# Block-sparse attention and a routed layer on one core: scores against one buffer of eight key blocks, shared values for 64 queries at once

## The chip, the core and the metric

The kernel runs on one core of a Trainium2 chip. Its engines run their own instruction streams in order: TensorE (PE, with its weight loads shown apart as PEld), VectorE (DVE), ScalarE (ACT), GpSimd (POOL) and SyncE (SP, which issues most of the transfers). The metric is the device time of one execution in microseconds, lower is better; three executions of the kernel before are given, and one of another execution's trace is read.

## The reference, cut to what matters

```python
# q, k, v: (4, 8, 768, 64), blocks of 32: 24 blocks; scale = 1/8
mask = np.abs(blk_i - blk_j) <= 1
mask = mask | (blk_i == 0) | (blk_j == 0) | (blk_i == 23) | (blk_j == 23)
for qb in range(24):
    for kb in sampled_blocks[qb]:                 # three random blocks a query block
        mask[qb * 32:(qb + 1) * 32, kb * 32:(kb + 1) * 32] = True
attn = softmax(np.where(mask, scale * q @ k.T, -1e9))
x = (attn @ v).transpose(0, 2, 1, 3).reshape(4, 768, 512)
# then, for each of the 4 batches: the 128 rows with the highest x @ w_gate
h = np.maximum(x[top] @ w1, 0.0); out[top] = x[top] + sigmoid(score) * (h @ w2)
```

A middle query block sees at most eight key blocks: the two blocks of its own unit, the first and the last block (these four are shared by both query blocks of a unit), and four of its own: three random ones and the outer neighbour. The first and the last query block see all 24.

## The kernel before

Work runs in 28 cycles, 14 for each pair of batches. In a pair, three **group** cycles (u = 0) hold query blocks 0 and 23 against a third of the keys each, and eleven **unit** cycles hold two neighbouring query blocks (e = 0, 1) with all heads of both batches (b = 0, 1). A cycle c on TensorE is, in program order:

- **turn**: 16 products with the identity that turn the probabilities `pr` of cycle c (128 by 128 each) into `ring` banks; ScalarE copies three of the four results to `pt`, VectorE the fourth;
- steps of the routed layer that are due at "m" (`spread`, `columns`, `column_sums`, `choose`, the first product `h`);
- `ahead(c + 1)`: **scores** of the next cycle for b = 0 and 1; VectorE takes their maxima (`m`, then `mx`, or `gx` in a group cycle), ScalarE the exponentials (`pr`);
- **outputs** of cycle c: probabilities (`pt`, the weights of the product) times values (65 columns, the last one is 1 and gives the sum);
- on VectorE `norm` (`z`, `x`, `j`), and the steps due at "e" (`expand` makes `r`, `rank` makes `cmp`, `select`).

Every fp32 product of scores and outputs is two matmuls and two weight loads on TensorE, a product with the identity is one of each. Scores use tiles of 64 by 32 of the array, outputs tiles of 128 by 32 (32 queries). A unit's scores are made of two products: one of 128 shared keys straight from `k` (the array `kb`), one of 128 own keys from `kr`, which GpSimd copies together two cycles ahead (`pool_work`, `keys`: six copies at offsets read from the table `koff`, and one for the neighbours). GpSimd also gathers the rows of own values `vr` by an indirect transfer; shared values `vs` come by SyncE.

The banks of `ring` go round three at a time, two banks each: two for turn, two for scores, one for outputs in each cycle. Small results of the routed layer (`bcast` of `spread`, `turnt`, `sums`, `selp`) share one bank, `tiny`; the order among its writers and readers is kept for the bank as a whole. `table()` and `rows_table()` turn the sampled blocks (`rb_i`) into `koff` and the row indices `vidx` on VectorE. Each engine keeps the order in which the program is written.

Of the kernel before, what the change touches and what calls it, by code (L numbers as in the profile page):

```python
# [7 lines left out]
F32 = mybir.dt.float32  # L8
# [4 lines left out]
ALU = mybir.AluOpType  # L13
# [28 lines left out]
def block_sparse_attention_moe(ctx, tc, qt, kt, vt, blocks, w_gate, w1, w2, outs):  # L42
# [144 lines left out]
    def rows_table():  # L187
# [4 lines left out]
        for pr in range(PAIRS):  # L192
# [14 lines left out]
    lim = const.tile([P, S], F32, name="lim")  # L207
    pool.memset(lim[:, 0:S - P], LIM0)
    limit = const.tile([P, P], F32, name="limit")
    pool.memset(limit, LIM0)  # L210
    pool.affine_select(lim[:, S - P:S], limit, pattern=[[-1, P]], compare_op=ALU.is_gt, fill=LIM,
                       base=0, channel_multiplier=1)
# [15 lines left out]

    krs, vrs, offs = {}, {}, {}

# [15 lines left out]
    def keys(n, e):  # L246
        pr, u = units[n]
        if e == 0:
            krs[n] = inp.tile([P, 2, NP, BP, KW], F32, tag="kr", name=f"kr{pr}_{u}", bufs=2)
        flat = kb[pr].rearrange("p j b c -> p (j b c)")  # L250
        for s in range(3):
            pool.tensor_copy(krs[n][:, e, s].rearrange("p b c -> p (b c)"), flat[:, ds(offs[n][3 * e + s], BP * KW)])
        if e:
            pool.tensor_copy(krs[n][:, :, 3], kb[pr][:, 2 * u - 2:2 * u + 2:3])

    def fetch_keys(n):
        if n < len(units):
            offsets(n)
            for e in range(2):
                keys(n, e)  # L260

# [10 lines left out]

    def grid(k, part, j, step, b, cols):
        a = k[part, j:j + 2, b, cols]
        return bass.AP(a.tensor, a.offset, [a.ap[0], [step * BP * KW, 2], a.ap[1], a.ap[2]])

    def scores(c, b):
        pr, u, t = c
        s = banks().rearrange("p g (h j k) -> p g h j k", h=2, k=BLK)
        q = qs[pr, u]  # L280
        for ph in range(2):
            for part in range(2 if u else 1):
                for e in range(2):
                    for p2 in range(2):
                        p, r0 = 2 * p2 + ph, 64 * p2 + 32 * e
                        cols = slice(p * BLK, (p + 1) * BLK)
                        for g in range(G):
                            half = slice(64 * g, 64 * g + 64)
                            if not u:
                                o, k = slice(0, 8), kb[pr][half, THIRD * t:THIRD * (t + 1), b, cols]  # L290
                            elif part == 0:
                                o, k = slice(0, 4), grid(kb[pr], half, 2 * u - 1, NB - 2 * u, b, cols)
                            else:
                                o, k = slice(4, 8), krs[number[c]][half, e, :, b, cols]
                            pe.matmul(s[r0:r0 + 32, g, ph, o], q[half, b, p, e], k,
                                      start=ph == 0 and part == 0, stop=ph == 1 and (part == 1 or not u),
                                      tile_position=(64 * g, r0), skip_group_check=True)
        return s.rearrange("p g h j k -> p g h (j k)")
# [50 lines left out]

    def outputs(c, b, o):  # L350
        pr, u, t = c
        for n in range(2):
            pt = pts.pop((c, b, n))
            for i in range(NP):
                for e in range(2):
                    for p2 in range(2):
                        h, r0 = p2 * NP + i, 64 * p2 + 32 * e
                        cols = slice(h * VW, (h + 1) * VW)
                        if not u:
                            v = vg[:, 2 * t + n, b, cols]  # L360
                        elif n == 0:
                            v = vss[number[c] % NVS][:, b, cols]
                        else:
                            v = vrs[number[c]][:, e, b, cols]
                        pe.matmul(o[r0:r0 + 32, b, i * VW:(i + 1) * VW], pt[:, i, r0:r0 + 32], v,
                                  start=n == 0 and i == 0, stop=n == 1 and i == NP - 1,
                                  tile_position=(0, r0), skip_group_check=True)

# [100 lines left out]
    def fetch(pr, b):  # L469
        ts = rout.tile([P, 2], F32, tag="ts", name=f"ts{pr}_{b}", bufs=4)  # L470
        vec.tensor_reduce(ts[:, 0:1], selp[:, b, 0:2], AX.X, ALU.add)
        it = R[pr]["it", b] = rout.tile([P, 1], U32, tag="it", name=f"it{pr}_{b}", bufs=4)
        vec.tensor_copy(it, ts[:, 0:1])
        xe = R[pr]["xe", b] = rout.tile([P, DM], F32, tag="xe", name=f"xe{pr}_{b}", bufs=4)
        pool.indirect_dma_start(out=xe[:], out_offset=None, in_=outs[BP * pr + b][:, :],
                                in_offset=bass.IndirectOffsetOnAxis(ap=it[:, 0:1], axis=0))
        vec.tensor_reduce(ts[:, 1:2], selp[:, b, 2:5], AX.X, ALU.add)
        R[pr]["ts", b] = ts
# [46 lines left out]


    n, per = len(cycles), NU + 2
    due = {}
# [17 lines left out]
    for pr in range(PAIRS):  # L546
        for t in range(NT):
            c = pr * per + 2 + 2 * t + 1
            if c == n - 1:
                break  # L550
            at(c, "e", expand, pr, t)
            at(c + 1, "m", spread, pr, t)
            at(c + 2, "m", columns, pr, t)
            at(c + 2, "m", rank, pr, t, 0)
            at(c + 2, "e", rank, pr, t, 1)
            at(c + 3, "m", column_sums, pr, t)
            if t % 2:
                at(c + 3, "p", parts, t - 1, t + 1, pr)
# [17 lines left out]

    done = None
    table()
    rows_table()

    def ahead(c):
# [9 lines left out]
    ahead(cycles[0])  # L591
    fetched = [0, 0]

    def pool_work(c):
        m = [number.get(cycles[i]) if i < n else None for i in (c + 1, c + 2)]
        if m[0] is not None and fetched[0] <= m[0]:
            rows(m[0], 0)
        if m[1] is not None:
            offsets(m[1])
            keys(m[1], 0)  # L600
        if m[0] is not None and fetched[0] <= m[0]:
            rows(m[0], 1)
            fetched[0] = m[0] + 1
        if m[1] is not None:
            keys(m[1], 1)

    for c in range(n):
# [11 lines left out]
        for b in range(BP):  # L619
            for k in range(2):  # L620
                turned(cy, b, pms[b], k)
        run(c, "m")
        if c + 1 < n:
            ahead(cycles[c + 1])
        o = banks()
        for b in range(BP):
            outputs(cy, b, o)
        norm(cy, o)
# [7 lines left out]
    expand(last, t)  # L636
    run(n, "m")
    assert not due
# [10 lines left out]
    for b in range(BP):  # L649
        select(last, b)  # L650
        choose(last, b)
        fetch(last, b)
        y(0, 1, 2 + 3 * b, 5 + 3 * b)
    for b in range(BP):
        put(0, b)
        gate(last, b)
# [53 lines left out]
```

## Time and profile before

| what | value |
|---|---|
| three executions | 395.23, 390.95, 394.15 us; median 394.15 us |
| the profiled execution | 391.02 us, of which the span is 389.2 us |
| mean granted clock of TensorE over the span | 0.904 of 2.4 GHz |
| share of busy time | PE 72%, weight loads 58%, DVE 50%, ACT 37%, POOL 33% |
| the chain that ended last | PE 49%, issue 24%, DVE 11%, ACT 6%, DMA 6% |
| transfers | 64.03 MB, 164 GB/s on average |

Busy shares are means over stages with different limits. "Issue" in the chain is time in which the engine waited for nothing that the profile shows. A row of the timeline or chain gives start and duration in us, a trailing bracket the idle time before it and what ended it.

### The profile page before, as it was taken

The numbers are of one execution on the slowest core, as the hardware profiler recorded it, in microseconds if no ns is written. First come the engines' busy times: TensorE is split into PE (matmuls) and PEld (weight loads), VectorE is DVE, ScalarE is ACT, GpSimd is POOL, SyncE is SP. The second block draws the span as 40 slices with busy tenths as digits, with TensorE's granted clock in tenths as the row PEclk, the third lists the DMA queues.
The fourth block names the chain that finished last, engine by engine and source line by source line (L and its number), as shares of the span: only waits on it lengthen the run. The fifth ranks groups of instructions, "written<-read, shape, count | busy, mean of one in ns | idle before, by whom it ended". The sixth has DMA issues, their size and how long they took to land.

```text
span 389.2 us, 17183 instructions
## 1 busy us (share of the span) xinstructions
PE 280.5 (72%) x7612; PEld 226.0 (58%) x7612; DVE 195.4 (50%) x580; ACT 144.6 (37%) x346; POOL 127.9 (33%) x251
## 2 busy tenths in 40 slices
PE   6197778585594584968676668658868968798992
PEld 5175666574484473757565457657666857347730
DVE  0655867455553463576676647463633556550000
ACT  1265454453513442455554434344323344002100
POOL 3170445423551355321136325532522530230000
PEclk9599999799866997899899978889969989999998
DMA  6994267949659977256637876773615532121000
GB/s 254 368 298 155 73 194 208 280 120 288 197 151 280 290 198 254 42 155 198 187 80 221 262 212 189 171 218 115 187 39 162 165 117 57 29 66 42 2 27 28
DMA packets 25083, 64.03 MB, mean 164 GB/s; under 512 B 3760, under 2 KB 10160, under 8 KB 24240
## 3 DMA queue, kind: packets, MB, share of 16 engines
q1 hardware_dynamic: 18032, 37.39, 32.6%
q0 software_dynamic: 6976, 25.53, 21.7%
q8 instruction: 60, 0.98, 1.1%
q14 instruction: 15, 0.12, 0.1%
HBM read 55.57 MB, written 7.34 MB: 162 GB/s over the span
## 4 chain that ended last, share of the span: by engine, by line
PE 49%; issue 24%; DVE 11%; ACT 6%; DMA 6%; SPq 2%; POOL 1%; POOLq 0%; ACTq 0%; DVEq 0%
PE ring L61 40%; PE mid L61 6%; ACT pr L61 4%; PE tiny L61 3%; DMA rb_i<-blocks 2%; DVE m L61 2%; DMA w2s<-w 2%; ACT pt_None L61 2%; SPq L61 2%; DMA vs<-vt 2%; DVE pt_None L61 1%; DVE cmp L61 1%; DVE x L61 1%; DVE j L61 1%; DVE r L61 1%
## 5 line engine op out<-in xcount | busy, mean ns | idle before, releaser
L61 ACT ACTIVATE pr_None<-ring,mx 128x256 f32<-128x256 f32 x176 | 67.1, 486 | 64.1 <-DVE mx L61 59.2
L61 POOL DMA_INDIRECT vr<-vt,vidx x44 | 42.5, 965 | 137.6 <-PE ring L61 132.9
L61 POOL COPY kr<-k 128x256 f32 (+1 forms) x154 | 67.2, 474 | 43.9 <-PE ring L61 22.0
L61 DVE TENSOR_REDUCE m_None<-ring 128x2 f32<-128x512 f32 x88 | 56.5, 683 | 33.8 <-PE ring L61 33.8
L61 PE MATMUL ring<-ident,pr_None 128*128 128x128 f32 x352 | 55.7, 323 | 6.9 <-issue 6.9
L61 PE MATMUL ring<-k,q 64*32 64x128 f32 (+1 forms) x1792 | 56.8, 307 | 4.0 <-issue 2.2
L61 ACT COPY pt_None<-ring 128x512 f32<-128x512 f32 x66 | 35.2, 592 | 64.0 <-PE ring L61 61.4
L61 PEld LDWEIGHTS ring<-ident,pr_None 128*128 128x128 f32 x352 | 49.2, 169 | 10.0 <-issue 8.3
L61 PE MATMUL ring<-vs,pt_None 128*32 128x65 f32 x1408 | 35.6, 235 | 23.8 <-issue 23.7
L61 PE MATMUL ring<-vr,pt_None 128*32 128x65 f32 x1408 | 36.8, 241 | 21.3 <-issue 21.3
L61 PE MATMUL ring<-kr,q 64*32 64x128 f32 x1408 | 45.3, 281 | 4.4 <-issue 4.3
L61 PEld LDWEIGHTS ring<-vr,pt_None 128*32 128x32 f32 x1408 | 29.9, 124 | 26.2 <-issue 26.2
L61 PEld LDWEIGHTS ring<-vs,pt_None 128*32 128x32 f32 x1408 | 27.3, 118 | 26.5 <-issue 25.9
L61 PEld LDWEIGHTS ring<-k,q 64*32 64x32 f32 x1792 | 33.7, 108 | 13.8 <-issue 10.6
L61 PEld LDWEIGHTS ring<-kr,q 64*32 64x32 f32 x1408 | 29.4, 110 | 7.2 <-issue 7.1
L61 DVE TENSOR_SCALAR z<-ring 128x8 f32<-128x8 f32 x22 | 3.6, 166 | 57.6 <-PE ring L61 57.6
L61 ACT ACTIVATE pr<-ring,gx 128x256 f32<-128x256 f32 x48 | 18.6, 479 | 30.8 <-DVE gx L61 30.8
L61 PE MATMUL ring<-ident,pr 128*128 128x128 f32 x96 | 15.6, 315 | 13.4 <-ACT pr L61 13.4
L61 DVE COPY pt_None<-ring 128x512 f32<-128x512 f32 x22 | 15.2, 689 | 19.5 <-ACT pt_None L61 19.5
L61 PE MATMUL ring<-w2s,ht 128*128 128x512 f32 x48 | 21.8, 599 | 0.9 <-DVE xe L61 0.9
L61 PEld LDWEIGHTS ring<-ident,pr 128*128 128x128 f32 x96 | 12.4, 160 | 16.2 <-issue 9.8
L61 DVE CUSTOM_DVE_ANT_0 j<-x,wg_i 128x256 f32<-128x256 f32 x48 | 20.4, 424 | 0.8
(99 smaller groups left out, 298.3 us busy)
## 6 DMA issues: line engine op xcount, KB each, us to landing
vs<-vt SPq DMA_DIRECT2D x28, 260.0 KB
q<-qt SPq DMA_DIRECT2D x24, 256.0 KB
out<-x SPq DMA_DIRECT2D x88, 64.0 KB
vg<-vt SPq DMA_DIRECT2D x4, 1040.0 KB
k<-kt SPq DMA_DIRECT2D x4, 1024.0 KB
k<-kt SPq DMA_DIRECT2D x2, 1152.0 KB
k<-w SPq DMA_DIRECT2D x4, 512.0 KB
w2s<-w SPq DMA_DIRECT2D x4, 512.0 KB
```

Source lines behind the costliest of these rows:

```text
L61: i = getattr(self.engine, name)(*args, **kw)
```

## The change

The four shared key blocks of a unit now lie in the same buffer as the own ones: `kr` has twelve blocks (own unit 0 to 1, first and last 2 to 3, then four for each query block). ScalarE copies the unit's two blocks two cycles ahead (`own_keys`); GpSimd copies the first and last block once for each buffer and pair of batches. A score product then takes 256 keys, by an access pattern that steps from blocks 0 to 3 to those of its query block. In outputs, where both query blocks share the values (`n == 0`, and all of a group cycle), one product takes 64 queries; a unit's shared values for both batches come first, then its own values. `spread` and `column_sums` move from "m" to a new place "s", behind `ahead(c + 1)`. `table()` and `rows_table()` come behind the first cycle's scores and maxima. At the end, `put(0, 0)` moves between the last two selections, with three buffers for `xe` rather than four. `lim` is set in place.

```diff
@@ start of the program
-    table()
-    rows_table()
...
     ahead(cycles[0])
+    table()
+    rows_table()
@@ buffers of keys
-    krs, vrs, offs = {}, {}, {}
+    NKR = 2
+    krs = [const.tile([P, 3 * NP, BP, KW], F32, name=f"kr{i}") for i in range(NKR)]
+    kr_pair = [None] * NKR
+    vrs, offs = {}, {}
@@ def keys(n, e)
-            pool.tensor_copy(krs[n][:, e, s].rearrange("p b c -> p (b c)"), flat[:, ds(offs[n][3 * e + s], BP * KW)])
+            pool.tensor_copy(kr[:, NP + NP * e + s].rearrange("p b c -> p (b c)"),
+                             flat[:, ds(offs[n][3 * e + s], BP * KW)])
         if e:
-            pool.tensor_copy(krs[n][:, :, 3], kb[pr][:, 2 * u - 2:2 * u + 2:3])
+            pool.tensor_copy(kr[:, 2 * NP - 1:3 * NP:NP], kb[pr][:, 2 * u - 2:2 * u + 2:3])
+
+    def own_keys(n):
+        pr, u = units[n]
+        if kr_pair[n % NKR] != pr:
+            kr_pair[n % NKR] = pr
+            pool.tensor_copy(krs[n % NKR][:, 2:4], kb[pr][:, NB - 1:NB + 1])
+        act.copy(krs[n % NKR][:, 0:2], kb[pr][:, 2 * u - 1:2 * u + 1])
@@ def scores(c, b)
+            for e in range(2):
+                for p2 in range(2):
+                    p, r0 = 2 * p2 + ph, 64 * p2 + 32 * e
+                    cols = slice(p * BLK, (p + 1) * BLK)
+                    for g in range(G):
+                        half = slice(64 * g, 64 * g + 64)
+                        if u:
+                            k = eight(krs[number[c] % NKR], half, e, b, cols)
+                        else:
+                            k = kb[pr][half, THIRD * t:THIRD * (t + 1), b, cols]
+                        pe.matmul(s[r0:r0 + 32, g, ph], qs[pr, u][half, b, p, e], k, start=ph == 0, stop=ph == 1,
+                                  tile_position=(64 * g, r0), skip_group_check=True)
@@ def outputs(c, b, o, n)
+        both = n == 0 or not u
+        for i in range(NP):
+            for e in range(1 if both else 2):
+                for p2 in range(2):
+                    h, r0 = p2 * NP + i, 64 * p2 + 32 * e
+                    r1 = r0 + (64 if both else 32)
...
+                    pe.matmul(o[r0:r1, b, i * VW:(i + 1) * VW], pt[:, i, r0:r1], v,
+                              start=n == 0 and i == 0, stop=n == 1 and i == NP - 1,
+                              tile_position=(0, r0), skip_group_check=True)
@@ the block scores' steps
-            at(c + 1, "m", spread, pr, t)
+            at(c + 1, "s", spread, pr, t)
...
-            at(c + 3, "m", column_sums, pr, t)
+            at(c + 3, "s", column_sums, pr, t)
@@ for c in range(n)
         run(c, "m")
+        if c + 2 < n and cycles[c + 2][1]:
+            own_keys(number[cycles[c + 2]])
         if c + 1 < n:
             ahead(cycles[c + 1])
+        run(c, "s")
         o = banks()
-        for b in range(BP):
-            outputs(cy, b, o)
+        for k in range(2):
+            for b in range(BP):
+                outputs(cy, b, o, k)
@@ fetch, and the end of the program
-        xe = R[pr]["xe", b] = rout.tile([P, DM], F32, tag="xe", name=f"xe{pr}_{b}", bufs=4)
+        xe = R[pr]["xe", b] = rout.tile([P, DM], F32, tag="xe", name=f"xe{pr}_{b}", bufs=3)
...
         choose(last, b)
+        if b == 0:
+            put(0, 0)
         fetch(last, b)
         y(0, 1, 2 + 3 * b, 5 + 3 * b)
+    put(0, 1)
     for b in range(BP):
-        put(0, b)
         gate(last, b)
```

On TensorE, cycle 8 (row names with 6: cycle 8's `pt`; with 7: the next cycle's queries and keys; `cmp_1` and `r_2`: the routed layer's steps 1 and 2). Before:

```order
L61 LDWEIGHTS cmp_1_1752
L61 MATMUL tiny<-one,cmp_1_1752 128x1
L61 LDWEIGHTS cmp_1_1752 [waits DVE_49]
L61 MATMUL tiny<-one,cmp_1_1752 128x1
L61 MATMUL tiny<-r_2_1919,ones 128x256 [waits DVE_49]
L61 MATMUL ring_75<-k_78,q_7_1480 32x128 [waits DMAHW7_49]
L61 MATMUL ring_75<-k_78,q_7_1480 32x128 x7
L61 MATMUL ring_75<-kr_7_1716,q_7_1480 32x128 [waits Pool_49]
L61 MATMUL ring_75<-kr_7_1716,q_7_1480 32x128 x7
L61 MATMUL ring_75<-k_78,q_7_1480 32x128 x8
L61 MATMUL ring_75<-kr_7_1716,q_7_1480 32x128 x8
L61 MATMUL ring_73<-k_78,q_7_1480 32x128 [waits Activation_49]
```

and now:

```order
L61 MATMUL ring_75<-kr_185,q_7_1210 32x256 [waits DMAHW7_49,DVE_49,Pool_49]
L61 MATMUL ring_75<-kr_185,q_7_1210 32x256 x15
L61 MATMUL ring_73<-kr_185,q_7_1210 32x256 [waits Activation_49]
L61 MATMUL ring_73<-kr_185,q_7_1210 32x256 x15
L61 LDWEIGHTS cmp_1_1433
L61 MATMUL tiny<-one,cmp_1_1433 128x1
L61 LDWEIGHTS cmp_1_1433 [waits DVE_49]
L61 MATMUL tiny<-one,cmp_1_1433 128x1
L61 MATMUL tiny<-r_2_1553,ones 128x256 [waits DVE_49]
```

The scores of one batch took four groups of products of 128 keys and take one run of 16 products of 256 keys; `column_sums` and `spread`, which stood ahead of the scores, stand behind both batches' scores and ahead of the outputs.

On VectorE at the same place (`rk` reads what `column_sums` left in `tiny`), before:

```order
L61 TENSOR_TENSOR r_2_1919<-sp_187,d_184 128x128 [waits DVE_49]
L61 COPY pt_6_None_1_1976<-ring_74 128x512 [waits Activation_49]
L61 SCALAR_TENSOR_TENSOR rk_1034<-tiny,rk_1034 128x2 [waits PE_49]
L61 TENSOR_REDUCE m_7_None_2015<-ring_75 128x2 [waits PE_49]
L61 TENSOR_REDUCE m_7_None_2015<-ring_75 128x2
L61 TENSOR_SCALAR mx_7_0_2018<-m_7_None_2015 128x4 [waits DVE_49]
L61 TENSOR_REDUCE m_7_None_2052<-ring_73 128x2 [waits PE_49]
L61 TENSOR_REDUCE m_7_None_2052<-ring_73 128x2
L61 TENSOR_SCALAR mx_7_1_2055<-m_7_None_2052 128x4 [waits DVE_49]
```

and now:

```order
L61 TENSOR_TENSOR r_2_1553<-sp_187,d_182 128x128 [waits DVE_49]
L61 COPY pt_6_None_1_1609<-ring_74 128x512 [waits Activation_49]
L61 TENSOR_REDUCE m_7_None_1628<-ring_75 128x2 [waits PE_49]
L61 TENSOR_REDUCE m_7_None_1628<-ring_75 128x2
L61 TENSOR_SCALAR mx_7_0_1631<-m_7_None_1628 128x4 [waits DVE_49]
L61 TENSOR_REDUCE m_7_None_1649<-ring_73 128x2 [waits PE_49]
L61 TENSOR_REDUCE m_7_None_1649<-ring_73 128x2
L61 TENSOR_SCALAR mx_7_1_1652<-m_7_None_1649 128x4 [waits DVE_49]
L61 SCALAR_TENSOR_TENSOR rk_860<-tiny,rk_860 128x2 [waits PE_49]
L61 TENSOR_SCALAR z_6_1719<-ring_74 128x8 [waits PE_49]
```

`rk` stood ahead of the maxima `m` of the next cycle and stands behind all of them.

On TensorE, the outputs of that cycle before:

```order
L61 MATMUL ring_74<-vs_84,pt_6_None_0_1970 32x65 [waits DMAHW0_49,Activation_49]
L61 MATMUL ring_74<-vs_84,pt_6_None_0_1970 32x65 x15
L61 MATMUL ring_74<-vr_6_1701,pt_6_None_1_1972 32x65 [waits DMASW2_49]
L61 MATMUL ring_74<-vr_6_1701,pt_6_None_1_1972 32x65
L61 MATMUL ring_74<-vr_6_1701,pt_6_None_1_1972 32x65 [waits DMASW3_49]
L61 MATMUL ring_74<-vr_6_1701,pt_6_None_1_1972 32x65 x13
L61 MATMUL ring_74<-vs_84,pt_6_None_0_1974 32x65 x16
L61 MATMUL ring_74<-vr_6_1701,pt_6_None_1_1976 32x65 x16
```

and now:

```order
L61 MATMUL ring_74<-vs_84,pt_6_None_0_1603 64x65 [waits DMAHW0_49,Activation_49]
L61 MATMUL ring_74<-vs_84,pt_6_None_0_1603 64x65 x7
L61 MATMUL ring_74<-vs_84,pt_6_None_0_1607 64x65 x8
L61 MATMUL ring_74<-vr_6_1383,pt_6_None_1_1605 32x65 [waits DMASW2_49]
L61 MATMUL ring_74<-vr_6_1383,pt_6_None_1_1605 32x65
L61 MATMUL ring_74<-vr_6_1383,pt_6_None_1_1605 32x65 [waits DMASW3_49]
L61 MATMUL ring_74<-vr_6_1383,pt_6_None_1_1605 32x65 x13
L61 MATMUL ring_74<-vr_6_1383,pt_6_None_1_1609 32x65 x16
```

The 32 products on shared values (`vs`, for 32 queries each) have become 16 for 64 queries, all ahead of the 32 on own values (`vr`). Over the program the listing holds 1248 products fewer: 704 of scores, 352 on `vs` and 192 on `vg`.

## Rows read from the trace of the kernel before

**Rows 1.** The profile page: span, busy time of the engines with the number of their instructions, TensorE's granted clock in 40 equal slices (tenths of full speed), the queue that brings instructions (packets, MB, share), and the chain that ended last by engine.

```profile
span 389.2 us, 17183 instructions
...
PE 280.5 (72%) x7612; PEld 226.0 (58%) x7612; DVE 195.4 (50%) x580; ACT 144.6 (37%) x346; POOL 127.9 (33%) x251
...
PEclk9599999799866997899899978889969989999998
...
q8 instruction: 60, 0.98, 1.1%
...
PE 49%; issue 24%; DVE 11%; ACT 6%; DMA 6%; SPq 2%; POOL 1%; POOLq 0%; ACTq 0%; DVEq 0%
```

**Rows 2.** Who waited for whom, on TensorE: engine and tile, what it waited for, us in total, times, longest.

```profile
PE ring L61 <- issue: 63.5, 38, 5.5
PE ring L61 <- ACT pr L61: 13.4, 9, 9.3
PE tiny L61 <- DVE rk L61: 7.1, 5, 1.5
...
PE tiny L61 <- DVE r L61: 2.6, 3, 1.0
```

**Rows 3.** The chain that ended last, in order of time, early and at the two longest pauses: start, us, what, number of instructions (matmuls).

```profile
41.15 1.69 issue
42.84 3.89 PE ring L61 x127
46.73 1.00 issue
47.73 2.19 PE ring L61 x127
49.93 1.37 issue
...
116.32 5.46 issue
...
280.51 4.94 issue
```

**Rows 4.** Busy time by stretch, for three single cycles (the third of the program, the tenth, and the last unit cycle of the first pair): stretch, its length, busy us (number) of PE, PEld, DVE, ACT, POOL, granted clock, DMA share, GB/s.

```profile
35.60:43.90 8.30, 6.25 (x274) 5.45 (x273) 6.26 (x12) 5.82 (x17) 3.46 (x8) 1.00 0.11 15
109.20:124.00 14.80, 9.34 (x277) 8.38 (x275) 6.45 (x18) 4.68 (x11) 4.94 (x9) 0.73 0.87 230
161.50:169.40 7.90, 6.63 (x217) 5.22 (x211) 6.84 (x21) 3.80 (x10) 5.25 (x9) 1.00 0.65 172
```

**Rows 5.** The same view for three stages: cycles 5 to 11, cycles 17 to 21, and what follows the last cycle's start. Columns as in rows 4.

```profile
61.90:145.60 83.70, 57.57 (x1931) 49.65 (x1925) 45.14 (x131) 33.29 (x80) 35.93 (x67) 0.86 0.76 222
...
198.60:258.00 59.40, 41.56 (x1390) 35.66 (x1388) 34.79 (x110) 25.48 (x61) 22.19 (x39) 0.87 0.72 207
...
326.10:389.20 63.10, 49.72 (x325) 29.94 (x316) 15.36 (x57) 6.37 (x14) 7.93 (x10) 0.98 0.11 34
```

**Rows 6.** The timeline of TensorE in a group cycle of the second pair, in which no pause fell: start, us, form, number.

```profile
173.47 0.70 PE L61 MATMUL tiny<-r,ones 128*128 128x256 f32 x2 [1.35 <-DVE rk L61]
174.10 1.96 PE L61 MATMUL ring<-k,q 64*32 64x256 f32 x64
175.99 2.05 PE L61 MATMUL ring<-vg,pt 128*32 128x65 f32 x128
178.52 1.09 PE L61 MATMUL ring<-ident,pr 128*128 128x128 f32 x8 [0.49 <-ACT pr L61]
```

**Rows 7.** The timeline of VectorE in the same cycle.

```profile
172.65 0.69 DVE L61 COPY pt<-ring 128x512 f32<-128x512 f32 x1 [0.49 <-ACT pt L61]
173.26 0.16 DVE L61 SCALAR_TENSOR_TENSOR rk<-tiny,rk 128x8 f32<-128x8 f32 x1
175.30 1.29 DVE L61 TENSOR_REDUCE m<-ring 128x2 f32<-128x512 f32 x2 [1.89 <-PE ring L61]
```

**Rows 8.** The timeline of the first cycle, TensorE and VectorE: the first scores, the table's first and last step, the first maxima, and the next cycle's.

```profile
6.47 1.96 PE L61 MATMUL ring<-k,q 64*32 64x256 f32 x64 [1.58 <-DMA k<-kt]
...
10.91 0.20 DVE L61 CAST rb<-rb_i 128x72 f32<-128x72 int32 x1 [9.96 <-DMA rb_i<-blocks]
...
15.40 0.26 DVE L61 TENSOR_SCALAR vidx<-own 128x22 int32<-128x22 f32 x2
15.57 1.28 DVE L61 TENSOR_REDUCE m<-ring 128x2 f32<-128x512 f32 x2
...
22.85 1.28 DVE L61 TENSOR_REDUCE m<-ring 128x2 f32<-128x512 f32 x2
```

**Rows 9.** The costliest groups of the page: busy us, mean ns of one, then the idle time before them and what ended it.

```profile
L61 ACT COPY pt_None<-ring 128x512 f32<-128x512 f32 x66 | 35.2, 592 | 64.0 <-PE ring L61 61.4
L61 PEld LDWEIGHTS ring<-ident,pr_None 128*128 128x128 f32 x352 | 49.2, 169 | 10.0 <-issue 8.3
L61 PE MATMUL ring<-vs,pt_None 128*32 128x65 f32 x1408 | 35.6, 235 | 23.8 <-issue 23.7
...
L61 PEld LDWEIGHTS ring<-vs,pt_None 128*32 128x32 f32 x1408 | 27.3, 118 | 26.5 <-issue 25.9
```

**Rows 10.** The timeline near the end: a run of the second product, and the sum that `put` makes.

```profile
346.35 2.82 PE L61 MATMUL ring<-w2s,ht 128*128 128x512 f32 x6
...
349.21 0.75 DVE L61 SCALAR_TENSOR_TENSOR xe<-ring,ge,xe 128x512 f32<-128x512 f32 x1 [1.35 <-PE ring L61]
```

More of the change, by code (lines that the diff above doesn't have):

```diff
@@ L207, in block_sparse_attention_moe @@
     lim = const.tile([P, S], F32, name="lim")
[L208 to L211, printed above, removed]
+    pool.memset(lim, LIM0)
+    pool.affine_select(lim[:, S - P:S], lim[:, S - P:S], pattern=[[-1, P]], compare_op=ALU.is_gt, fill=LIM,
                        base=0, channel_multiplier=1)
@@ L247, in keys @@
         pr, u = units[n]
-        if e == 0:
-            krs[n] = inp.tile([P, 2, NP, BP, KW], F32, tag="kr", name=f"kr{pr}_{u}", bufs=2)
+        kr = krs[n % NKR]
         flat = kb[pr].rearrange("p j b c -> p (j b c)")
         for s in range(3):
-            pool.tensor_copy(krs[n][:, e, s].rearrange("p b c -> p (b c)"), flat[:, ds(offs[n][3 * e + s], BP * KW)])
+            pool.tensor_copy(kr[:, NP + NP * e + s].rearrange("p b c -> p (b c)"),
+                             flat[:, ds(offs[n][3 * e + s], BP * KW)])
         if e:
-            pool.tensor_copy(krs[n][:, :, 3], kb[pr][:, 2 * u - 2:2 * u + 2:3])
[L256 to L260, printed above, removed]
+            pool.tensor_copy(kr[:, 2 * NP - 1:3 * NP:NP], kb[pr][:, 2 * u - 2:2 * u + 2:3])
[5 more added lines that the diff above has]
+        act.copy(krs[n % NKR][:, 0:2], kb[pr][:, 2 * u - 1:2 * u + 1])
     cycles = []
@@ L271, in block_sparse_attention_moe, with eight @@
     sps = [const.tile([P, BP, NU], F32, name=f"sp{i}") for i in range(PAIRS)]
-    def grid(k, part, j, step, b, cols):
-        a = k[part, j:j + 2, b, cols]
-        return bass.AP(a.tensor, a.offset, [a.ap[0], [step * BP * KW, 2], a.ap[1], a.ap[2]])
+    def eight(k, half, e, b, cols):
+        a = k[half, 0:NP, b, cols]
+        return bass.AP(a.tensor, a.offset, [a.ap[0], [NP * (1 + e) * BP * KW, 2], a.ap[1], a.ap[2]])
     def scores(c, b):
@@ L279, in scores @@
         s = banks().rearrange("p g (h j k) -> p g h j k", h=2, k=BLK)
-        q = qs[pr, u]
         for ph in range(2):
[L282 to L297, printed above, removed]
+            for e in range(2):
[10 more added lines that the diff above has]
+                                  tile_position=(64 * g, r0), skip_group_check=True)
         return s.rearrange("p g h j k -> p g h (j k)")
@@ L348, in turned, with outputs @@
             act.copy(pt, pm[:, n])
-    def outputs(c, b, o):
+    def outputs(c, b, o, n):
         pr, u, t = c
[L352 to L367, printed above, removed]
+        pt = pts.pop((c, b, n))
+        both = n == 0 or not u
[4 more added lines that the diff above has]
+                    r1 = r0 + (64 if both else 32)
+                    cols = slice(h * VW, (h + 1) * VW)
+                    if not u:
+                        v = vg[:, 2 * t + n, b, cols]
+                    elif n == 0:
+                        v = vss[number[c] % NVS][:, b, cols]
+                    else:
+                        v = vrs[number[c]][:, e, b, cols]
+                    pe.matmul(o[r0:r1, b, i * VW:(i + 1) * VW], pt[:, i, r0:r1], v,
+                              start=n == 0 and i == 0, stop=n == 1 and i == NP - 1,
+                              tile_position=(0, r0), skip_group_check=True)
     def norm(c, o):
@@ L573, in block_sparse_attention_moe @@
             at(c + 6 + f // 2, "m", relu, 0, f - 1)
-    done = None
-    table()
-    rows_table()
     def ahead(c):
@@ L591, in block_sparse_attention_moe @@
     ahead(cycles[0])
-    fetched = [0, 0]
+    table()
+    rows_table()
     def pool_work(c):
         m = [number.get(cycles[i]) if i < n else None for i in (c + 1, c + 2)]
[L596 to L605, printed above, removed]
+        for e in range(2):
+            if m[0] is not None:
+                rows(m[0], e)
+            if m[1] is not None:
+                if e == 0:
+                    offsets(m[1])
+                keys(m[1], e)
     for c in range(n):
@@ L636, in block_sparse_attention_moe @@
     expand(last, t)
-    run(n, "m")
+    run(n, "s")
     assert not due
```

## The prediction

> **What bounds the kernel now.** I read the page first. TensorE is busy 72% of a span of 389.2 us, VectorE 50%, and the chain that ended last has 49% TensorE and 24% "issue" [rows 1]. A quarter of the time, then, goes by while the engine at the end of the chain waits for nothing that the profile names. So I went to the waits of TensorE next: the largest is "issue" ahead of products into `ring`, 63.5 us in 38 pieces; waits for exponentials are 13.4 us, for VectorE's `rk` 7.1 us [rows 2]. Then the chain in order of time, to see where the pauses stand: they come after runs of 127 or 128 matmuls, in the middle of a row of equal products [rows 3]. The instruction queue moved 0.98 MB in 60 packets [rows 1], 16.3 KB each; 7612 matmuls and 7612 weight loads make that 64 bytes an instruction, so a packet is 256 instructions: 128 matmuls and their loads. The pauses have the period of the packets. I read them as TensorE running dry: it uses up a packet before the next has come. Where nothing else is late, one comes every 3.6 us (resumed at 47.73, then at 51.30); at the two longest pauses TensorE stood for 5.46 and 4.94 us [rows 3].
>
> A single cycle shows the demand. In a cycle free of pauses the scores take 1.96 us and the outputs 2.05 us [rows 6]. A unit cycle's scores are 128 matmuls, its outputs 128, with as many loads: 256 instructions in each 2 us, where a packet takes 3.6 us. The third view is the clock: cycles without long pauses run at the full 2.4 GHz (granted clock 1.00), with TensorE busy 6.25 and 6.63 us; a cycle with a 5.46 us pause has a granted clock of 0.73, a mix of 1.2 and 2.4 GHz, and TensorE is busy 9.34 us for the same products [rows 3, 4]. A pause so costs twice.
>
> **The change part by part.** All sums are made against the profiled execution, 391.0 us, which is 0.8% under the median of the three shown (394.15) and at their lower end.
>
> *Fewer instructions.* 1248 products go; each is two matmuls and two loads, so 4992 of 15,224 instructions, and 60 packets become 40.5. Per unit cycle TensorE has 176 matmuls rather than 272. The array's own time hardly moves: 64 score matmuls of 256 keys take 1.96 us [rows 6], and the 128 of 128 keys lie inside the same 6.25 us cycle [rows 4]. A unit cycle without pauses needs about 6 us (16 turns at some 2 us, as 8 take 1.09, scores 2, outputs 2) [rows 6]. That is 6 x 256 / 544 = 2.8 us of work per packet now and 6 x 256 / 352 = 4.4 us then. Setting the extra 1.5 us against each pause, the many of 1.0 to 1.7 us vanish and those of 5 us shrink to 3.5 [rows 3]. Summed over the pauses about 25 of 63.5 us stay [rows 2], and with two thirds of the packets 17 us. That would give back 46 us. I take 41, since some pauses lie under exponentials or transfers that end late anyway. Bounds: 63 if every pause goes, 21 if a packet keeps its mean pause and only a third of them go.
>
> *The clock.* In cycles 5 to 11 TensorE is busy 57.57 us, 8.2 a cycle, at a granted clock of 0.86, and in cycles 17 to 21 8.3 a cycle at 0.87 [rows 5], against 6.25 to 6.6 at 1.00 [rows 4]: some 13 us and 8 us above, about 22 with the other stages. Only the part that is on the path comes back, and only where pauses go. I take 8 us; bounds 0 and 20.
>
> *The first maxima ahead of the table.* The scores of the first cycle end at 8.4 us, but VectorE takes their maxima only at 15.57, behind a table that it could start at 10.91, when the sampled blocks had landed [rows 8]. Now both pairs of maxima run before 10.9, the table ends at 15.6 as before, and the exponentials, turns and copies of the first cycle go on beside it. VectorE's copy of `pt` follows the table (0.69 us [rows 7]), so the next maxima can start at 16.3 rather than 22.85 [rows 8]: 6.5 us off the start. The offsets for GpSimd come when they came before. If keys or values were late there the gain is less; bounds 3 and 8.
>
> *`spread` behind the scores.* Seven of the eleven steps inside the cycles have `column_sums` and its `rk` just ahead. Before, TensorE waited 1.35 to 1.5 us for `rk` there [rows 2, 6], since VectorE first copied `pt`. Now `rk` stands behind four maxima (two pairs of 1.29 us [rows 7] and their scalings). From the end of the turns `pt` takes 1.4 us and the maxima 2.9, so `rk` is done after 4.6 us; the scores need 2 us of it. The wait becomes about 2.4 us: +0.95 us, seven times, +6.7. In the other four places TensorE waited for `r` (2.6 us in three waits [rows 2]), which two score runs now cover: -3. Net +3.5; the exponentials, started earlier, may cover it, or the outputs behind it may pass it on whole: bounds 0 and +8.
>
> *64 queries at once.* No row shows a tile of 128 by 64. Its weight load lies between that of 32 columns (118 ns) and of 128 (169 ns) [rows 9]. Two such tiles lie side by side where four did; four start a product every 16 ns (2.05 us / 128 [rows 6]), 64 ns a tile, so two would start one every 32 ns, and half as many products take the same time. If loads stop hiding behind the other tile, the row nearest to that is the full-width turn: 8 in 1.09 us, or 136 ns each [rows 6]. I take 0, as the tiles of 32 already hide loads longer than their spacing; the far end is the slow rival below.
>
> *One more change of tile shape.* A unit cycle now goes from tiles of 64 to tiles of 32 columns within its outputs. From scores to outputs the row shows no gap beyond the last product's end (174.10 + 1.96, next at 175.99) [rows 6]. The price is at most one product's length, 0.235 us [rows 9]; 22 times, +5. Bounds 0 and 5. The Trainium skill ("TensorEngine Tiling (Array Packing)", Key Properties) says that changing the tiling mode drains TensorE, a rule against this change; the row agrees with a drain no longer than one product. By it the term is 5, without it 0.
>
> *Hidden at no cost.* ScalarE's `own_keys` is one more copy of 512 columns (592 ns) in each unit cycle, behind the copies to `pt`, while it waits for maxima: it idled 64.0 us ahead of such copies [rows 9]. Without that cover it would delay exponentials by 0.6 us a cycle, 13 us. GpSimd's four extra copies are two per pair of batches, and POOL is busy 33% [rows 1]. At the end `put(0, 0)` moves 0.75 us of VectorE work and a GpSimd transfer ahead of a gather whose rows are needed only after the next 2.82 us run of products [rows 10]: 0. The last 63.1 us hold no such pause (PE busy 49.7, clock 0.98) [rows 5] and stay.
>
> *What is late next.* Transfers: they took 76% of the 83.7 us of cycles 5 to 11 and 72% of the 59.4 us of cycles 17 to 21 [rows 5], so these cannot fall below 63.6 and 42.8 us. My sum takes some 16 and 12 us from them and stays above. VectorE is busy 6.3 to 6.8 us a cycle [rows 4], which stops cycles near 7.5.
>
> **Sum:** 391.0 - 41 - 8 - 6.5 + 3.5 + 5 = 344 us, 13% less.
>
> **The rivals.**
> A. *The pauses do not shrink.* Faster cycles crowd the transfers, each packet comes later, and only the number of packets falls: -21 for pauses, -3 for the clock. For it: the longest pauses lie in the stages with most transfers [rows 3, 5]. 391.0 - 21 - 3 - 6.5 + 8.5 = 369 us.
> B. *Nearly all of it comes back.* Pauses and slow clock both go: 391.0 - 60 - 15 - 7 + 3 = 312 us. Against it: the floor of the transfers.
> C. *The pauses are not instructions.* Something in the array or the banks has that period by chance; then only the start moves: 391.0 - 6.5 + 8.5 = 393 us. Against it: runs of 127 in the middle of equal products. The Trainium skill stands on this side ("Runtime: NRT & Kernel Launch", Instruction fetch mechanics): it says that crossing a 16 KiB boundary is mostly hidden because dispatch is slower than the fill. The trace disagrees with it here, with 63.5 us of pauses at that period [rows 2, 3].
> D. *Slower: the 64-query products run one after the other.* 704 + 384 = 1088 matmuls of this kind remain; at 136 ns rather than 32 each they add 113 us: 344 + 113 = 457 us. It decides against the change from 32 + 47 / 1088 = 75 ns each. For it: 64 columns have no row. Against it: tiles of 32 columns and of 64 rows both run side by side [rows 6].
>
> **How the numbers follow.** My forecast (330 to 356 us) gets 0.62, A 0.17, B 0.11, C 0.05, D 0.05. The predicted time is that of the likeliest, 344. The range leaves out C and D and takes in A and B: 312 to 370. One per cent, 4 us, is about what a measurement of this kernel can tell from no change. Faster by more than that: forecast, A and B, 0.90. Within it: C, 0.05. Slower: D, 0.05.
>
> **What would show it.** Right: some 40 instruction packets; far fewer and shorter "issue" waits ahead of `ring`; a granted clock of 0.95 or more; the second cycle's maxima near 16.3 us; `vs` products 32 ns apart; TensorE waiting 2 to 3 us for `rk` seven times. Wrong: pauses of the old mean size at every packet (A), pauses unmoved in place and sum (C), or `vs` runs of 32 longer than 2.4 us (D).

## The result, and the profile after

The changed kernel takes 334.56 us (median of four executions, 330.96 to 339.02) where the kernel before takes 392.66 us beside it (four, 390.95 to 395.23): a ratio of 0.8485, 95% interval 0.838 to 0.859. Two more series of the study gave 337.81 us (0.8691, 0.8587 to 0.8795) and 334.68 us (0.8565, 0.8507 to 0.8624). The prediction was 344 us within 312 to 370. A ratio leaves out executions in a slower state, so it can differ a little from that of the medians. The profiled execution took 335.87 us, span 334.1 us; against the profiled one of before (391.02) that is 55.2 us less.

The profile page of the changed kernel, the lines that answer to [rows 1]:

```profile
span 334.1 us, 12192 instructions
...
PE 272.9 (82%) x5116; PEld 199.1 (60%) x5116; DVE 196.8 (59%) x580; ACT 153.6 (46%) x368; POOL 130.9 (39%) x254
...
PEclk9999999999599979979997799979979997999998
...
q8 instruction: 40, 0.66, 0.8%
...
PE 48%; DVE 22%; issue 14%; ACT 9%; DMA 3%; POOL 1%; POOLq 0%; SPq 0%; ACTq 0%; DVEq 0%
```

TensorE has 5116 matmuls rather than 7612, and 40 packets of instructions came rather than 60. In the chain, "issue" went from 24% to 14%, and VectorE, which stands next in it, from 11% to 22%. The mean clock is 0.949 rather than 0.904.

Not all "issue" in these chains is a pause of TensorE. Some 30 us of it, before as after, lie near the end, where the chain stands on GpSimd's last transfers while TensorE computes. Before:

```profile
351.22 23.40 issue
...
375.83 6.77 issue
```

and after:

```profile
295.94 23.85 issue
...
321.01 6.77 issue
```

Without them "issue" fell from 64 to 17 us, so the "quarter of the time" of the prediction was a sixth.

Who waited for whom on TensorE (us in total, times, longest), to set beside [rows 2]:

```profile
PE tiny L61 <- DVE rk L61: 12.8, 6, 2.5
PE ring L61 <- issue: 10.5, 7, 2.9
PE ring L61 <- ACT pr_None L61: 7.9, 17, 0.9
PE ring L61 <- ACT pr L61: 6.8, 9, 1.6
```

The pauses ("issue") are down from 63.5 us in 38 pieces to 10.5 us in 7. The wait for `rk` is up from 7.1 to 12.8 us: it is now the largest of all.

The chain in order of time at the two longest pauses that are left (start, us, what, matmuls), to set beside [rows 3]:

```profile
76.19 4.63 PE ring L61 x124
80.81 2.79 issue
...
112.72 3.81 PE ring L61 x127
116.53 2.93 issue
```

They still follow runs of 124 and 127 matmuls (127 and 127 in TensorE's timeline, which has the few that the chain leaves out), and 2.79 and 2.93 us stand where it was 5.46 and 4.94.

Busy time by stretch (length, busy us and number of PE, PEld, DVE, ACT, POOL, granted clock, DMA share, GB/s): cycles 5 to 11, cycles 17 to 21 and the end, which answer to [rows 5]; 8 us about each of the two pauses; and the moment at which TensorE resumes after a wait for `rk` of 2.49 us (130.00 to 145.74 ends with that wait):

```profile
52.40:120.30 67.90, 53.15 (x1257) 39.52 (x1253) 45.27 (x131) 36.62 (x88) 36.40 (x67) 0.94 0.88 274
164.80:210.20 45.40, 39.62 (x909) 28.61 (x909) 35.87 (x112) 27.64 (x68) 23.65 (x42) 0.92 0.87 256
269.20:334.10 64.90, 51.62 (x290) 30.69 (x284) 15.23 (x57) 5.90 (x12) 7.96 (x10) 0.95 0.11 33
76.00:84.00 8.00, 5.02 (x143) 3.79 (x143) 5.73 (x18) 5.12 (x13) 5.53 (x12) 1.00 1.01 337
112.00:120.00 8.00, 4.45 (x152) 3.36 (x148) 4.53 (x10) 3.61 (x10) 3.17 (x7) 0.95 1.03 352
...
130.00:145.74 15.74, 11.94 (x315) 9.03 (x303) 13.40 (x40) 7.92 (x19) 5.26 (x9) 1.00 0.54 146
...
146.37:149.92 3.55, 3.55 (x65) 3.43 (x65) 0.00 (x0) 1.17 (x5) 0.00 (x0) 0.52 0.97 239
```

The stages show where the 55 us came from. A cycle starts with the first product of its turns; the lengths are differences of those starts in the two traces:

| stage | before | after | less |
|---|---|---|---|
| up to cycle 5 | 61.9 | 52.4 | 9.5 |
| cycles 5 to 11 | 83.7 | 67.9 | 15.8 |
| cycles 12 to 16 | 53.0 | 44.5 | 8.5 |
| cycles 17 to 21 | 59.4 | 45.4 | 14.0 |
| cycles 22 to 26 | 68.1 | 59.0 | 9.1 |
| cycle 27 and the end | 63.1 | 64.9 | -1.8 |

The stages with the most pauses gave the most, and the end, which had none, took 1.8 us more. The DMA share in cycles 5 to 11 rose from 0.76 to 0.88 for the same bytes, and about the two pauses that are left the transfers are at their full share.

TensorE's timeline (start, us, form, number): the first outputs of the program, a unit cycle's outputs, and a group cycle with its wait for `rk`:

```profile
17.18 2.09 PE L61 MATMUL ring<-vg,pt 128*64 128x65 f32 x64 [0.96 <-DVE pt L61]
...
107.18 1.15 PE L61 MATMUL ring<-vs,pt_None 128*64 128x65 f32 x32
108.26 1.13 PE L61 MATMUL ring<-vr,pt_None 128*32 128x65 f32 x64
...
141.00 1.96 PE L61 MATMUL ring<-k,q 64*32 64x256 f32 x64
142.89 0.35 PE L61 MATMUL tiny<-one,cmp 128*128 128x1 bf16 x8
145.74 0.70 PE L61 MATMUL tiny<-r,ones 128*128 128x256 f32 x2 [2.49 <-DVE rk L61]
146.37 3.62 PE L61 MATMUL ring<-vg,pt 128*64 128x65 f32 x64
```

VectorE's timeline: the first maxima, the table's first and last step, the second cycle's maxima, to set beside [rows 8]; then the maxima ahead of that `rk`:

```profile
10.36 1.29 DVE L61 TENSOR_REDUCE m<-ring 128x2 f32<-128x512 f32 x2
...
11.76 0.19 DVE L61 CAST rb<-rb_i 128x72 f32<-128x72 int32 x1
...
16.28 0.26 DVE L61 TENSOR_SCALAR vidx<-own 128x22 int32<-128x22 f32 x2
16.44 0.69 DVE L61 COPY pt<-ring 128x512 f32<-128x512 f32 x1
17.04 1.28 DVE L61 TENSOR_REDUCE m<-ring 128x2 f32<-128x512 f32 x2
...
142.34 1.28 DVE L61 TENSOR_REDUCE m<-ring 128x2 f32<-128x512 f32 x2
...
143.93 1.28 DVE L61 TENSOR_REDUCE m<-ring 128x2 f32<-128x512 f32 x2
...
145.52 0.16 DVE L61 SCALAR_TENSOR_TENSOR rk<-tiny,rk 128x8 f32<-128x8 f32 x1
```

64 matmuls for 64 queries each take 2.09 us, 33 ns apiece, where 128 for 32 queries took 2.05 [rows 6]. A unit's outputs, 96 matmuls in two shapes, run from 107.18 to 109.39: 2.21 us. The second cycle's maxima start at 17.04 rather than 22.85.

### The profile page after: what moved, and what is told of

Read it like the earlier page. It is cut to its first block, busy times and chain, and to the rows that moved or that the text cites. A ratio compares the mean times of both kernels' runs of the same rounds, so it can differ in the third digit from the quotient of the medians.

```text
span 334.1 us, 12192 instructions
## 1 busy us (share of the span) xinstructions
PE 272.9 (82%) x5116; PEld 199.1 (60%) x5116; DVE 196.8 (59%) x580; ACT 153.6 (46%) x368; POOL 130.9 (39%) x254
## 4 chain that ended last, share of the span: by engine, by line
PE 48%; DVE 22%; issue 14%; ACT 9%; DMA 3%; POOL 1%; POOLq 0%; SPq 0%; ACTq 0%; DVEq 0%
PE ring L61 37%; PE mid L61 7%; DVE m_None L61 7%; ACT pr_None L61 4%; PE tiny L61 4%; ACT pr L61 3%; DVE m L61 3%; DMA k<-kt 2%; DMA out<-x 1%; ACT pt L61 1%; DVE acc L61 1%; DVE x L61 1%; DVE pt L61 1%; DVE mx L61 1%; DVE j L61 1%
## 5 line engine op out<-in xcount | busy, mean ns | idle before, releaser
L61 POOL COPY kr<-k 128x256 f32 (+1 forms) x158 | 70.1, 481 | 32.0 <-DMA k<-kt 14.6
L61 PE MATMUL ring<-kr,q 64*32 64x256 f32 x1408 | 51.8, 399 | 3.8 <-issue 3.4
L61 PE MATMUL ring<-ident,pr_None 128*128 128x128 f32 x352 | 47.3, 284 | 8.6 <-ACT pr_None L61 7.9
L61 PEld LDWEIGHTS ring<-ident,pr_None 128*128 128x128 f32 x352 | 39.5, 145 | 14.1 <-ACT pr_None L61 11.5
L61 PE MATMUL ring<-vr,pt_None 128*32 128x65 f32 x1408 | 28.5, 234 | 5.3 <-issue 5.1
L61 PEld LDWEIGHTS ring<-vs,pt_None 128*64 128x64 f32 x704 | 24.9, 147 | 9.3 <-issue 5.9
L61 PE MATMUL ring<-vs,pt_None 128*64 128x65 f32 x704 | 28.7, 235 | 2.0 <-issue 1.3
L61 PEld LDWEIGHTS ring<-vr,pt_None 128*32 128x32 f32 x1408 | 24.0, 118 | 9.0 <-issue 7.5
L61 ACT ACTIVATE pr<-ring,gx 128x256 f32<-128x256 f32 x48 | 18.7, 477 | 23.0 <-DVE gx L61 12.8
L61 DVE SCALAR_TENSOR_TENSOR xe<-ring,ge,xe 128x512 f32<-128x512 f32 x3 | 2.3, 751 | 33.3 <-PE ring L61 33.3
L61 PE MATMUL tiny<-r,ones 128*128 128x256 f32 x24 | 9.1, 463 | 14.9 <-DVE rk L61 12.8
L61 DVE TENSOR_REDUCE m<-ring 128x2 f32<-128x512 f32 x24 | 15.4, 681 | 7.9 <-PE ring L61 7.8
```

The source lines that it names most:

```text
L61: i = getattr(self.engine, name)(*args, **kw)
```

## The experiments

The theory was the prediction's: TensorE runs dry of instructions, and fewer of them, spread thinner, end the pauses. Its rivals: the shapes of the products themselves save the time, or the moves of `spread` and of the table do. All times are medians; differences are taken within a series on one chip.

**First series: the products split again, the order of the changed kernel kept.** Before 389.18 us there.

The changed kernel once more, `after_again`:

> The changed kernel itself beside the three above, as the anchor on this chip: 330-339 us by each theory, 40 packets, issue waits ahead of ring about 10 us.

337.81 us, ratio 0.8691 (0.8587 to 0.8795): in its range. Its pauses are 13.5 us in 10 pieces.

`u_scores`: a unit's score product of 256 keys becomes two of 128 from the same buffer.

```diff
-                            k = eight(krs[number[c] % NKR], half, e, b, cols)
...
+            for part in range(2 if u else 1):
...
+                                o = slice(NP * part, NP * (part + 1))
+                                k = four(krs[number[c] % NKR], half, NP * (1 + e) * part, b, cols)
```

> The changed kernel, but each unit score product of 256 keys split again into two of 128 from the same buffer: 704 products (2816 instructions, 11 packets) come back, nothing else moves. Packet theory (TensorE runs dry between instruction packets; the change gained some 57 us by 20 fewer packets, near 2.5 us each with the clock): 51 packets, issue waits ahead of ring back from 10.5 to 25-35 us, granted clock down to about 0.92, time 350-368 us. Rival (the gain came from the new order, the start and the one key buffer, not from the number of instructions): the array's time for the scores is the same, so 335 us within 4.

373.78 us (0.9584, 0.9477 to 0.9692), 36.0 us above the changed kernel: more than the theory's range, in its direction, and so are the pauses (25 to 35 us expected). Of its profile, the page's line on instructions, the wait, and a stretch of the chain:

```profile
q8 instruction: 51, 0.84, 1.0%
```

```profile
PE ring L61 <- issue: 46.8, 36, 4.8
```

```profile
63.44 4.45 PE ring L61 x127
67.89 2.20 issue
```

11 packets more bring 33.3 us more of pauses, 3.0 us each, again behind runs of 127 matmuls such as this one.

`u_outputs`: products of 32 queries throughout, so that outputs have one shape of tile only.

```diff
-        both = n == 0 or not u
+        both = False
```

> The changed kernel, but shared values in products of 32 queries again, in the same new order: 544 products (2176 instructions, 8.5 packets) come back and the tile shape no longer changes within the outputs. Packet theory: 49 packets, issue waits 20-30 us, time 345-362 us. Rival (shape: a product of 64 queries is slower on the array or the change of shape drains it, so taking both away gains): 325-334 us. Second rival (order and start brought the gain): 335 within 4.

357.43 us (0.9167, 0.9057 to 0.9277), 19.6 us above: in the theory's range. The rival, by which the shape was dear, expected a gain, and falls. 49 packets came, as expected, and the wait is just above the 20 to 30 us expected:

```profile
PE ring L61 <- issue: 31.3, 22, 5.1
```

`u_both`: both edits together, which brings back the 7612 matmuls and the 60 packets of before, with everything else as changed.

> Both splits together: the number of TensorE instructions is that of the kernel before, but the one key buffer, the new order of spread, of the outputs and of the table stay. Packet theory: 60 packets, issue waits 50-70 us, granted clock 0.89-0.92, time 380-390 us, the kernel before less the start. Rival (order, start and buffer): 335-345 us.

389.24 us against 389.18 us before (four executions of 384.09 to 390.80, seven of 385.77 to 395.93), no difference. The whole gain is gone, and the pauses are back; below them stand a unit cycle's scores, in a cycle where no pause cuts them:

```profile
PE ring L61 <- issue: 59.4, 42, 4.8
```

```profile
276.17 2.03 PE L61 MATMUL ring<-kr,q 64*32 64x128 f32 x128
```

From the changed kernel to this one pauses rise by 45.9 us and the time by 51.4. In the two halves it was 33.3 and 36.0, 17.8 and 19.6. Time follows the pauses at 1.08 to 1.12 for one by the medians (1.07 to 1.16 by which executions are compared), however they are brought back. The array's own time does not explain it: 128 score matmuls of 128 keys take 2.03 us where 64 of 256 take 1.96 [rows 6], 1.5 us in 22 cycles. So the gain goes with the number of instructions, and all else that the change does, the moves of `spread` and the table with it, shows no gain together, within a few us.

The record of transfers ties the pauses to the packets. Before, 29 of the 38 pauses, all of 0.69 us or more, end 1.21 to 1.60 us after an instruction packet has landed, and in `u_both` the 24 of 0.64 us or more end 1.21 to 1.66 us after one. For the longest [rows 3] the packet moved from 118.54 to 120.22, and TensorE resumed at 121.79. The packets of these two traces move in 0.88 to 1.78 us each; the longest pauses had begun up to 2.4 us before theirs set out, so there it is the start of the packet that is late.

**Second series: the moves, one at a time.** Before 392.44 us there; the changed kernel was not run beside them, so these stand by their ratios to before.

`u_spread`: both steps back at their old place ahead of the scores.

```diff
-            at(c + 1, "s", spread, pr, t)
+            at(c + 1, "m", spread, pr, t)
...
-            at(c + 3, "s", column_sums, pr, t)
+            at(c + 3, "m", column_sums, pr, t)
...
-    run(n, "s")
+    run(n, "m")
```

> The changed kernel, but spread and column_sums back at m, ahead of the scores. My step (the wait for rk grew from 1.45 to 2.4 us in seven places, four other waits went): this undo gains 0-8 us, so 327-335 us, with waits of 1.4 us for rk ahead of spread and four waits for r. Rival (the move helped, because the scores and with them maxima and exponentials start earlier): 337-350 us.

328.96 us (0.8472, 0.8308 to 0.8635). `rk` now costs 9.4 us in 7 waits, and the exponentials of unit cycles 14.3 us, where the changed kernel's three traces have 7.9 to 11.3. The mean ratio of the changed kernel's three series is 0.858, which puts the gain near 4 us, but the interval holds 0 as well as 10. The rival, by which the move was a gain, is not borne out. Of the four waits for `r` that were expected back one came, of 0.5 us.

`u_table`: the table first again.

```diff
+    table()
+    rows_table()
...
     ahead(cycles[0])
-    table()
-    rows_table()
```

> The changed kernel, but the table of sampled blocks ahead of the first maxima again on VectorE. My step: 6.5 us (3 to 8) come back at the start, 338-343 us, and the second cycle's turns begin near 26 us rather than 20.3. Rival (the first values and keys arrive too late for the earlier start to last): within 2 us of the changed kernel.

340.79 us (0.872, 0.8517 to 0.8923), inside the range expected, some 5 us above 0.858 of the same before, with an interval as broad. VectorE's timeline at the start, in this kernel:

```profile
15.78 1.28 DVE L61 TENSOR_REDUCE m<-ring 128x2 f32<-128x512 f32 x2
...
24.22 1.29 DVE L61 TENSOR_REDUCE m<-ring 128x2 f32<-128x512 f32 x2 [0.84 <-PE ring L61]
```

The second cycle's maxima start at 24.22 rather than 17.04 us: the start itself loses 7.2 us. The second cycle's turns begin at 28.4 (near 26 expected, 20.3 in the changed kernel).

`x_sums_late`: since the wait for `rk` is the largest that is left, `column_sums` goes behind the outputs of its cycle, which do not need it.

```diff
-            at(c + 3, "s", column_sums, pr, t)
+            at(c + 3, "o" if c + 3 < n else "s", column_sums, pr, t)
...
                 outputs(cy, b, o, k)
+        run(c, "o")
         norm(cy, o)
```

> The changed kernel, with column_sums behind the outputs, ahead of norm: spread no longer stands behind rk and the four maxima. My step (spread's wait for rk, 12.8 us in TensorE's waits, is on the path in seven cycles): the wait goes, 322-330 us. Rival (the cycles are bound by maxima and exponentials on VectorE and ScalarE, and the wait was cover): 332-338 us. A second rival: column_sums then waits for ScalarE's copy of spread's result, behind eight exponentials, and holds up norm: slower, 338-345 us.

322.64 us (0.8272, 0.8104 to 0.8439), as expected.

**Third series, more executions of each, the changed kernel beside them.** Before 390.76 us there.

`after_5`:

> The changed kernel unaltered, on the chip of the next three, so that these are compared with it directly. Expected 331 to 339 us as in its two earlier series.

334.68 us (0.8565, 0.8507 to 0.8624). The wait that the next two are about, in its trace:

```profile
PE tiny L61 <- DVE rk L61: 15.3, 7, 2.4
```

`x_sums_late_5`, the last kernel again:

> The changed kernel with column_sums and its rk behind the outputs, on one chip with the changed kernel. If TensorE's seven waits for rk (12.8 us in the trace of the changed kernel) are on the path that sets the end: 320 to 328 us, 8 us or more under the changed kernel. If the lower time of the first series came from the chip: the same as the changed kernel within 3 us.

324.46 us (0.8308, 0.8262 to 0.8354), 10.2 us under the changed kernel, and the intervals are apart. The wait for `rk` is gone, and the mean clock is 0.960 rather than 0.941. What stands there is a wait for `sb`, which ScalarE copies behind exponentials:

```profile
PE ring L61 <- issue: 10.9, 8, 2.6
PE tiny L61 <- ACT sb L61: 9.3, 6, 2.0
```

A wait of 9.3 us took the place of one of 15.3 us, and yet 10.2 us are won. I read it so: most of the 9.3 us lies where TensorE's next products, the turns, would wait for exponentials anyhow.

`x_spread_m_sums_late` tests that reading: `spread` back ahead of the scores, so that `sb` is early, with `column_sums` late.

```diff
-            at(c + 1, "s", spread, pr, t)
+            at(c + 1, "m", spread, pr, t)
...
-            at(c + 3, "s", column_sums, pr, t)
+            at(c + 3, "o" if c + 3 < n else "s", column_sums, pr, t)
...
+        run(c, "o")
```

> spread back at its old place ahead of the scores, column_sums behind the outputs, a place later than in the changed kernel. column_sums would no longer wait for ScalarE's copy behind the exponentials (9.1 us in 7 waits in the run with column_sums late). If those waits are on the path: 314 to 320 us. If ScalarE's exponentials and VectorE's maxima cover them, as I think, since the next cycle's turns wait for exponentials anyway: 320 to 328 us, the same as column_sums late alone.

322.34 us (0.8258, 0.8208 to 0.8308): 2.1 us below, and the two intervals overlap. The wait for `sb` has left the list:

```profile
PE ring L61 <- ACT pr_None L61: 13.2, 33, 0.9
PE ring L61 <- issue: 10.5, 8, 3.9
PE ring L61 <- ACT pr L61: 8.9, 11, 1.5
PE tiny L61 <- DVE r L61: 4.8, 8, 1.2
```

Of the 9.3 us taken away some 2 came back, 6 at most by the ends of the intervals. In these two traces the rest went to exponentials (13.2 and 8.9 us, 22.1 together, where `x_sums_late_5` has 11.1 and 7.3, 18.4 together) and to `r` (4.8 us). Both kernels of this kind beat the kernel before and the changed one.

`own_twice`: the copy that the prediction put at nothing, doubled.

```diff
         act.copy(krs[n % NKR][:, 0:2], kb[pr][:, 2 * u - 1:2 * u + 1])
+        act.copy(krs[n % NKR][:, 0:2], kb[pr][:, 2 * u - 1:2 * u + 1])
```

> ScalarE's copy of the own two key blocks is issued twice in each unit cycle: the cost that the prediction set at nothing is doubled. If idle time of ScalarE ahead of the maxima hides it: the changed kernel's time within 3 us. If it delays the exponentials: 22 copies of 0.6 us, 13 us more, 344 to 352 us.

332.58 us (0.8496, 0.844 to 0.8551) beside 334.68: no cost. The group in its trace (count, busy us, mean ns, idle time before):

```profile
L61 ACT COPY kr<-k 128x512 f32<-128x512 f32 x44 | 27.4, 622 | 0.7
```

22 more copies of 622 ns are 13.7 us of ScalarE, and none of them shows in the time.

## Why the prediction was right, and by how much it was off

It forecast 344 us and 334.56 came. By its terms:

- **Pauses, -41, and clock, -8.** The mechanism is shown: `u_both` brings the instructions back and the time with them, and the pauses end behind packets. The size of the first was too small. The working left 17 us of pauses, and 10.5 are left (13.5 and 10.1 in the other two profiles), so that -53.0 stands where -46 was worked out and -41 taken. What failed is the scaling of the long ones. The 27 pauses of up to 1.76 us (24.9 us in all) were to vanish, and 5 are left, 4.8 us. The 11 of 2.31 us or more (38.6 us) were to shrink by 1.5 us each and to thin out by a third; they shrank so, to 2.93 us at the longest (forecast 3.5; 3.34 and 3.40 in the other two profiles), but only two are left. The clock rose, nearly as far as said (0.949, and 0.942 and 0.941 in the other two; forecast 0.95 or more). What it gave was not measured apart: the time moved by 1.08 to 1.12 us for each us of pause, which leaves 1.8 to 5.5 us for the clock and all else where 8 were taken. Pauses, clock and change of shape together were -44 in the sum; `u_both`, which undoes these three, measures -51.4 (-49 to -51 by which executions are compared). This is the term that was mis-sized.
- **Start, -6.5.** The second cycle's maxima moved by 5.8 us (17.04 for 22.85; forecast 16.3), and undoing the move costs some 5 us. The step held. The 0.7 us by which it missed belong to this execution: the chain shows its first scores as a run of 3.65 us from 6.68 (1.96 us before, [rows 8]), so the first maxima ended at 11.65 and the table began at 11.76, not at 10.91. In the other two traces of the changed kernel these scores take 1.96 us and the second cycle's maxima start at 16.22 and 16.05. Why this run was slow stays open.
- **`spread`, +3.5 (0 to 8).** The waits for `rk` came as worked out: up to 2.5 us each (forecast 2.4), behind four maxima, which end at 145.2 before `rk` at 145.52; no wait for `r` is left. `u_spread` puts the cost near 4 us, which agrees, with an interval broader than the bounds. The sum had -6.5 + 3.5 = -3 for the two moves; `u_both`, which equals the kernel before, would put them at 0, and its few executions cannot tell the two.
- **Change of tile shape, +5.** 2.21 us for a unit's outputs in two shapes against 2.05 in one [rows 6] (2.05 and 2.06 in `u_outputs`, where no pause falls): 0.16 us each, 22 times, 3.5 us. The Trainium skill's drain ("TensorEngine Tiling (Array Packing)", Key Properties) agrees with that row, as a cost that is there, and smaller than one matmul (0.235 us [rows 9]).
- **64 queries, 0.** 33 ns a matmul, as said (32); rival D is out. The term stood 0, and the row gives 0.04 us a group cycle.
- **The hidden copy, 0.** `own_twice` shows it. The row that the working cites [rows 9] is not the cover: it is idle time ahead of the copies to `pt`, in which ScalarE waits for TensorE's turns. Its wait for maxima, ahead of a unit's exponentials, was of about the same size before:

```profile
ACT pr_None L61 <- DVE mx L61: 59.2, 25, 4.2
```

- **The end, 0.** It takes 64.9 us (65.2 and 66.4 in the other two traces) rather than 63.1. In this trace 1.4 of the 1.8 us are one run of four matmuls behind a wait for `cmp`, 3.37 us from 276.81 where it took 1.96. No run undoes the moves at the end.
- **Transfers as the next floor.** The sum took some 16 and 12 us from cycles 5 to 11 and 17 to 21 and kept them above 63.6 and 42.8 us. They lost 15.8 and 14.0 and ended at 67.9 and 45.4. Rival B's 312 us did not come: these two stages kept 4.3 and 2.6 us above the forecast's floors, and some 10 us lay in the place of `column_sums` and its `rk`, for which the change made TensorE wait longer, as `x_sums_late_5` shows. The floors were not fixed, either: 0.88 of 67.9 us and 0.87 of 45.4 are 59.8 and 39.5 us.

Rival A (only the number of packets falls) is out with 7 pauses in 40 packets, where there were 38 in 60. Rival C falls with `u_both`. The Trainium skill's sentence on its side ("Runtime: NRT & Kernel Launch", Instruction fetch mechanics: crossing a 16 KiB boundary is mostly hidden) does not hold for a stretch of products as dense as these: 63.5 us of pauses were there [rows 2], and went with the instructions.

In short, the forecast's mechanisms held, and it gave 5 to 7 us too little for pauses, clock and shape. It forecast 47 us less; the three series of the changed kernel measure 51.4, 56.1 and 58.1 us less by their medians, so the miss is 4 to 11 us by series.

Three things stay open. Why a packet that is brought back costs 3.0 us in scores and 2.0 us in outputs (17.8 us for 9 packets) was not tried apart. What delays the start of a packet is not shown: that full transfers do it is read from two stretches, and no run took transfers away. And each run changed the number of instructions by dividing products; none added instructions alone.

## What to carry to other kernels

When "issue" pauses come after runs of one fixed length in the middle of equal products, count instructions, not engine time, and look whether each pause ends just behind an instruction packet: a product of twice the width that takes as long as two narrow ones halves the demand for instructions, which no view of busy time shows. A small step that waits on VectorE, put ahead of a long run of products, delays all of them; put it behind the run that does not need it, and look at which wait takes its place. Test a cost that is called hidden by doubling it.

## What the runs showed of the hardware that was not expected

- A wait can cost twice through the clock, as the pauses did. After 2.49 us of waiting for `rk` TensorE ran at a granted clock of 0.52, the lower of its two levels (1.2 GHz), from 146.37 to 149.92, having had 1.00 over the 15.74 us before; 64 matmuls took 3.62 us rather than 2.09. The same stands behind a wait of 1.51 us for `rk` (granted clock 0.50 over the 5.00 us from 86.30) and one of 2.71 us for `cmp` (0.58 over the 3.51 us from 276.69). After two other waits of 2.2 and 2.3 us in that trace (resumed at 106.55 and 127.83) the matmuls ran at their usual speed (32 in 1.15 us), so it does not come each time. The prediction priced this wait by its length alone.
- The granted clock of the whole span says little of what pauses cost: `u_outputs`, with 31.3 us of pauses, has 0.902, `u_scores`, with 46.8, has 0.924, and the slower kernel is the second. Over four executions they have 0.902 to 0.936 and 0.901 to 0.924.
